# Zero matmuls in TensorE's early gaps, and the outer products of k moved from POOL to DVE, in a planned attention and token-mixing kernel

## The chip, the cores and the metric

The kernel runs on one core of a Trainium2 chip. The metric is the device time of one execution in microseconds, as the median of several runs. PE is the matrix engine TensorE, PEld its weight loads, DVE the vector engine, ACT the scalar engine, POOL the GpSimd engine and SP the queue that issues loads and stores.

## The reference

Four batches, four heads, 1088 positions, 32 features a head; sketch matrices of 8 rows.

```python
def phi(x):                                   # x: batch, head, position, 32
    a = einsum('rd,bhsd->bhsr', S1, x);  b = einsum('rd,bhsd->bhsr', S2, x)
    return einsum('bhsi,bhsj->bhsij', a, b)   # flattened to 64
q_p, k_p = phi(q), phi(k)
kv = einsum('bhsf,bhsd->bhfd', k_p, v);  z = k_p.sum(axis=2)
attn = einsum('bhsf,bhfd->bhsd', q_p, kv) / (einsum('bhsf,bhf->bhs', q_p, z) + 1e-6)
x = attn, heads side by side                  # batch, 1088, 128
theta = x @ w_theta
y = einsum('ts,bsd->btd', w_tok_r, x * cos(theta)) + einsum('ts,bsd->btd', w_tok_i, x * sin(theta))
u = x + y
out = u + relu(u @ w_ch)
```

The denominator can come close to zero, so it is computed in several levels of split numbers, while the numerator is plain float32. The weights arrive as 64-bit numbers, which the kernel turns into float32 itself.

## The kernel before, in words

Positions lie in nine chunks of 128, taken in three groups of three (`NG` = 3, `GC` = 3).

- For each batch, keys are cut into a bf16 grid and remainders (stages `grid`, `keys`, `sums`, `rest`). Sums over positions are formed on PE. For batch 0 DVE forms the remainders; for batches 1 to 3 POOL subtracts (L684), held back by a one-element tile `gate`, which is copied (L1106) when batch 0's factor `nu` is there. `chain` (L757), first for batch 0 and then for batches 1 to 3 together, goes back and forth between DVE (`split`, `split_t`, `cut`) and PE and gives the factors of the denominator.
- `kfeatures` (L701) makes the key features: PE transposes k (L714), ACT copies (L717), PE multiplies by the block matrix `sbk` into a PSUM tile `kf`, ACT copies all of it (192 columns) to SBUF as `ks` (L727), POOL forms the outer products `kp` chunk by chunk (36 instructions, `outer`, L731), and PE sums `kp` against v into `kv`. `chain_out` makes the block-diagonal tile `kvbd` from it.
- `query_scale`, `query_slices`, `levels` and `outputs_x` do the same for the queries: transposes, two slices of q, level products on PE, denominator on DVE (`den`), outer products of q (DVE for batch 0, POOL for batches 1 to 3, by `QPOOL`), numerator on PE (`num`), the phase with sine and cosine on ACT and the products with x on DVE into `z` (`theta`).
- The token weights come as 17 rows of 1088 columns. Each is loaded as 64-bit words, converted by three ACT instructions (L610, L612, L614) and put together by two DVE instructions (L616, L618).
- `mix_row` multiplies `z` by the rows on PE, 17 steps a group: batch 0 has its three groups at once and goes row by row; for batches 1 to 3 groups go one after another, with two groups of batch 1 early. `mix_out` adds x, applies the last weights and stores.

The order in which each engine gets its instructions is not the order of the source. Every operation is registered with `op(engine, duration, function, writes, reads, due)`. `Layout.run` goes backwards from the outputs' due times to give each operation a due time and adds a number for its stage from the table `SHIFT`. `Layout.forward` then plays the program with the written durations: of the operations that could start next on an engine it takes the one with the earliest due time, hands out buffer slots (of PSUM, class `ps`, there are eight, of which four are kept back for operations that are due earlier), and models that POOL and DVE hinder each other at a shared port (`lk`). `Layout.issue` emits the result in that order; each engine works through its queue strictly in it. A change of a duration, a shift or the rules can thus move every instruction of every engine.

Of the kernel before, what the change touches and what calls it, by code (L numbers as in the profile page):

```python
# [14 lines left out]
I32 = mybir.dt.int32  # L15
# [41 lines left out]
}  # L57
LOAD_LEAD = 60.0
RAW_LEAD = 30.0
CHAINS = ((0,), (1, 2, 3))  # L60
QPOOL = (False, True, True, True)
QFIX = 2.006
# [18 lines left out]
class Layout:  # L81


    START = {"P": 1.3, "V": 0.8, "A": 0.7, "G": 1.3, "S": 0.5}
    ISSUE = 0.4
# [71 lines left out]
    def forward(self):  # L157
# [21 lines left out]
        def place(o):  # L179
            t = 0.0  # L180
            need = {}
            for b in o.bufs:
                if b.slot is None and b.cls is not None:
                    need.setdefault(b.cls, []).append(b)
            for c, bs in need.items():
                av = sorted(s[0] for s in slots[c] if s[1] is None)
                last = max((b.due, b.ops[0]) for b in bs)
                before = bisect.bisect_left(pending[c], last, key=lambda x: x[:2]) - len(bs) + 1
                if len(av) < len(bs) + min(max(before, 0), self.RESERVE[c]):
                    return None  # L190
                t = max(t, av[len(bs) - 1])
            return t

        while done < len(ops):
            pick = None
            for e in "PVAGS":
                cand = []
                for o in ready[e]:
                    t = max(free[e], o.ready, o.due - o.lead)
                    p = place(o)  # L200
                    if p is None:
                        continue
                    t = max(t, p)
                    if o.lk:
# [7 lines left out]
                t, o = min((c for c in cand if c[0] <= first + self.SLACK[e]), key=lambda c: (c[1].rank, c[1].i))  # L212
                if pick is None or t < pick[0]:
                    pick = (t, o)
            if pick is None:
                raise RuntimeError("no room: " + str([(o.eng, round(o.due), [b.name for b in o.bufs]) for e in "PVAGS"
                                                      for o in ready[e]]))
# [38 lines left out]
    def issue(self, pools):  # L256
        for o in self.order:
            for b in o.bufs:
                if b.ap is None:
                    b.ap = view(pools[b.cls](b.slot), b.shape, b.dt)  # L260
            o.fn()
# [33 lines left out]
def kernel(  # L295
# [107 lines left out]
    op("V", 1.0, constants, [hm, bdm, halfpi, steps, ups, ones], [])  # L403
    op("A", 1.6, lambda: A.activation(warm(), halfpi(), AF.Sin), [warm], [halfpi], due=0.0)
# [13 lines left out]
    if wide:  # L418
# [4 lines left out]
        op("A", 0.4 * H + 0.4, read_small, [st], [], due=-9.0, fly=2.0)  # L423
# [86 lines left out]
    op("G", 1.3, sliced, [cm, c16, cf], [sc, sf], lk=7)  # L510
# [24 lines left out]
    op("G", 0.5, blocks_k, [s32, sbk], [sp, hm], lk=2)  # L535
# [40 lines left out]
    op("G", 0.9, spread2, [sx2, psc], [s0, sc], lk=4)  # L576
# [26 lines left out]
    def weight(dst, dfn, src, n, due=None):  # L603
# [8 lines left out]
        op("A", 0.24 + n * 0.00105, lambda: A.activation(stp()[:, :, 1].bitcast(F16), words_of(raw(), n)[1].bitcast(F32),  # L612
                                                     AF.Copy, scale=2.0**-60), [(stp, 1)], [raw])
        op("A", 0.24 + n * 0.00105, lambda: A.activation(stp()[:, :, 0], words_of(raw(), n)[0].bitcast(U32), AF.Copy,  # L614
# [3 lines left out]
        op("V", n * 0.0012 + 0.08, lambda: tt(V, dfn().bitcast(I32), dfn().bitcast(I32),  # L618
# [16 lines left out]
    def key_sums(b):  # L635
# [25 lines left out]
        op("V", 0.3, key_steps, [(km, 0)], [(km, 1), steps], lk=1)  # L661
# [11 lines left out]
        for c in range(NC):  # L673
            op("P", 0.22, lambda c=c: levels_of(c), [(t, "l")], [kb])
        at("rest", b)
        kh = buf("big", (NC, HD), F32, "kh")
        for g in range(NG):
            x = slice(g * GC, (g + 1) * GC)
            if b == 0:
                vop(GW, lambda x=x: tt(V, r()[:, x], r()[:, x], kb()[:, 1, x], ALU.subtract), [(r, g)], [(kb, 1)], lk=1)  # L680
                vop(GW, lambda x=x: stt(kh()[:, x], r()[:, x], -0.5, kx()[:, x].rearrange("p c h d -> p c (h d)"),
                                        ALU.mult, ALU.add), [(kh, g)], [(r, g), kx], lk=1)
            else:
                op("G", 0.93, lambda x=x: tt(G, r()[:, x], r()[:, x], kb()[:, 1, x], ALU.subtract), [(r, g)],  # L684
                   [(kb, 1), gate], lk=1)
# [15 lines left out]
    def kfeatures(b):  # L701
# [3 lines left out]
        for g in range(NG):  # L705
# [3 lines left out]
            ks = buf("sm", (CH, 2 * R), F32, "ks")  # L709
# [17 lines left out]
            op("A", act(CH * 2 * R), lambda kf=kf, ks=ks: A.copy(ks().rearrange("p n r -> p (n r)"), kf()), [ks], [kf])  # L727

            at("kv", b)

            def outer(i, kp=kp, ks=ks):  # L731
                h = slice(i * H, (i + 1) * H)
                tt(G, kp()[:, h], bc(ks()[:, h, 0:R], 3, [P, H, R, R]), bc(ks()[:, h, R:2 * R], 2, [P, H, R, R]), ALU.mult)

            for i in range(GC):
                op("G", 0.64, lambda i=i, f=outer: f(i), [(kp, i)], [ks, gate], lk=1)
# [20 lines left out]
    def chain(bs):  # L757
# [3 lines left out]
        for b in bs:  # L761
# [10 lines left out]
            op("V", 1.25, split, [e0, e1], [t, kg[b], kg[b, 0]], lk=1)  # L772
# [135 lines left out]
    def levels(b):  # L908
# [43 lines left out]
        op("V", 0.75, finish_den, [dn], [(ep[b], 1)], lk=2)  # L952
# [5 lines left out]
    def outputs_x(b, lv, pool_qp):  # L958
# [3 lines left out]
        for g in range(NG):  # L962
# [54 lines left out]
            op("A", act(GW) + .08, lambda cs=cs: A.activation(cs()[:, 0], cs()[:, 0], AF.Sin, bias=halfpi(),  # L1017
                                                              scale=-TWO_PI), [(cs, 0)], [halfpi])
            op("A", act(GW) + .08, lambda cs=cs: A.activation(cs()[:, 1], cs()[:, 1], AF.Sin, scale=-TWO_PI), [(cs, 1)],  # L1019
# [77 lines left out]
    for bs in CHAINS:  # L1097
# [34 lines left out]
    with tc.manual_schedule():  # L1132
        L.issue(pools)
# [43 lines left out]
```

## Time and profile before

| | |
|---|---|
| median of 3 runs | 283.65 us (283.55 to 283.65) |
| the profiled execution | 284.34 us, of which the span is 282.6 us |
| busy | PE 253.1, DVE 162.2, ACT 142.8, POOL 77.4 us |
| mean granted clock of PE | 0.962 |

A row of the profile names a line, an engine, an operation and the tiles it writes and reads. Buffers of one class have one name: `big`, `zs`, `g`, `sm`, `hf`, `lv` are classes of SBUF buffers and `ps` is PSUM. Helpers record their own line: L372 is every matmul, L356 every tensor-tensor operation on DVE or POOL, L360 every tensor-scalar and L363 every scalar-tensor-tensor; L714, L898, L982, L1004 and L1070 are transposes. A float32 matmul appears as two instructions.

### The profile page before, as it was taken

The numbers are of one execution on the slowest core, as the hardware profiler recorded it, in microseconds if no ns is written. First come the engines' busy times: TensorE is split into PE (matmuls) and PEld (weight loads), VectorE is DVE, ScalarE is ACT, GpSimd is POOL, SyncE is SP. The second block draws the span as 40 slices with busy tenths as digits, with TensorE's granted clock in tenths as the row PEclk, the third lists the DMA queues.
The fourth block names the chain that finished last, engine by engine and source line by source line (L and its number), as shares of the span: only waits on it lengthen the run. The fifth ranks groups of instructions, "written<-read, shape, count | busy, mean of one in ns | idle before, by whom it ended". The sixth has DMA issues, their size and how long they took to land.

```text
span 282.6 us, 3841 instructions
## 1 busy us (share of the span) xinstructions
PE 253.1 (90%) x1447; PEld 187.9 (67%) x1447; DVE 162.2 (57%) x337; ACT 142.8 (51%) x231; POOL 77.4 (27%) x112
## 2 busy tenths in 40 slices
PE   3596898588599899997999999999999999999993
PEld 3495797467497767664776687657876755565762
DVE  1768769999799999899564078104652400010102
ACT  4569953367667898977898040334606700000101
POOL 0291024999954800085000000700042000000000
PEclk9999557999989999999999999999999999999999
DMA  7999924406404018441500012000000000010011
GB/s 260 388 420 422 409 84 159 160 0 247 154 0 160 1 16 302 143 175 44 198 2 0 0 52 58 0 23 0 2 28 23 2 0 0 0 30 0 1 54 52
DMA packets 9154, 28.77 MB, mean 102 GB/s; under 512 B 944, under 2 KB 5296, under 8 KB 6960
## 3 DMA queue, kind: packets, MB, share of 16 engines
q1 hardware_dynamic: 8928, 28.51, 27.2%
q8 instruction: 11, 0.18, 0.3%
q14 instruction: 7, 0.06, 0.1%
q10 hardware_dynamic: 208, 0.02, 0.1%
HBM read 26.30 MB, written 2.23 MB: 101 GB/s over the span
## 4 chain that ended last, share of the span: by engine, by line
PE 61%; DVE 16%; POOL 9%; ACT 7%; issue 3%; DMA 2%; SPq 0%; DVEq 0%; ACTq 0%
PE ps L372 56%; POOL g L356 5%; DVE big L356 4%; POOL big L356 3%; DVE big L360 2%; DMA big<-q_l 2%; ACT big L614 2%; ACT big L612 2%; DVE lv L356 2%; PE ps L982 2%; DVE sm L356 2%; PE ps L1070 1%; DVE big L363 1%; ACT big L610 1%; PE ps L1004 1%
## 5 line engine op out<-in xcount | busy, mean ns | idle before, releaser
L372 PE MATMUL ps<-big,zs 128*128 128x384 f32 (+1 forms) x408 | 128.6, 469 | 0.0
L372 PEld LDWEIGHTS ps<-big,zs 128*128 128x128 f32 x408 | 75.6, 190 | 42.7 <-issue 0.8
L356 POOL TENSOR_TENSOR g<-lv 128x256 f32<-128x256 f32 x27 | 20.4, 790 | 95.9 <-DVE lv L356 95.9
L1080 ACT ACTIVATE g<-ps 128x384 f32<-128x384 f32 (+2 forms) x16 | 6.2, 406 | 65.8 <-PE ps L372 65.8
L356 POOL TENSOR_TENSOR g<-sm 128x256 f32<-128x256 f32 x36 | 35.6, 1024 | 6.7 <-ACT sm L727 6.7
L356 DVE TENSOR_TENSOR g<-big,ps 128x384 f32<-128x384 f32 (+1 forms) x12 | 6.4, 530 | 52.5 <-PE ps L372 52.5
L356 DVE CUSTOM_DVE_ANT_0 big<-big,big 128x2176 uint16<-128x2176 uint16 x17 | 23.9, 1404 | 5.1 <-ACT big L614 4.6
L612 ACT ACTIVATE big<-zs 128x1088 f16<-128x1088 f32 (+1 forms) x18 | 24.8, 1380 | 0.0
L614 ACT ACTIVATE big<-zs 128x1088 int16<-128x1088 uint32 (+1 forms) x18 | 24.8, 1376 | 0.0
L986 ACT COPY g<-ps 128x384 f32<-128x384 f32 x24 | 10.3, 483 | 22.3 <-PE ps L982 20.6
L610 ACT ACTIVATE big<-zs 128x1088 f32<-128x1088 f32 x17 | 20.5, 1213 | 0.6 <-DMA zs<-w_tok 0.6
L372 PE MATMUL ps<-big,big 128*128 128x128 f32 x72 | 11.4, 318 | 7.9 <-DVE big L363 7.8
L372 PEld LDWEIGHTS ps<-big,big 128*128 128x128 f32 x72 | 10.1, 222 | 9.0 <-DVE big L363 9.0
L356 DVE TENSOR_TENSOR zs<-ps,g 128x768 f32<-128x768 f32 (+2 forms) x20 | 12.0, 630 | 6.2 <-ACT g L1019 6.1
L360 DVE TENSOR_SCALAR big<-big 128x1088 int32<-128x1088 int32 x17 | 14.8, 869 | 1.1 <-ACT big L610 1.1
L363 DVE SCALAR_TENSOR_TENSOR g<-g,ps 128x384 f32<-128x384 f32 x12 | 6.6, 552 | 14.8 <-ACT g L1013 14.8
L356 DVE TENSOR_TENSOR g<-g,ps 128x384 f32<-128x384 f32 (+2 forms) x16 | 6.9, 450 | 14.0 <-ACT g L1080 9.0
L372 PE MATMUL ps<-mf,big 128*128 128x96 f32 x72 | 14.4, 295 | 0.5 <-DVE big L356 0.5
L372 PE MATMUL ps<-sbk,g 128*128 128x64 f32 x72 | 13.9, 359 | 0.8 <-POOL sbk L356 0.8
L372 PEld LDWEIGHTS ps<-sbk,g 128*128 128x128 f32 x72 | 13.1, 273 | 1.3 <-POOL sbk L356 0.9
L372 PE MATMUL ps<-g,big 128*64 128x128 f32 x144 | 11.4, 293 | 2.5 <-POOL g L356 2.5
L714 PE MATMUL ps<-ident,big 128*128 128x128 f32 x36 | 8.1, 389 | 4.8 <-DMA big<-k_l 4.8
(163 smaller groups left out, 391.8 us busy)
## 6 DMA issues: line engine op xcount, KB each, us to landing
zs<-w_tok SPq DMA_DIRECT2D x17, 1088.0 KB, 6.1
big<-k_l SPq DMA_DIRECT2D x4, 576.0 KB, 10.0
big<-v_l SPq DMA_DIRECT2D x4, 576.0 KB, 6.3
big<-q_l SPq DMA_DIRECT2D x4, 576.0 KB, 5.2
out<-g SPq DMA_DIRECT2D x8, 192.0 KB, 2.1
out<-g SPq DMA_DIRECT2D x4, 128.0 KB, 1.8
zs<-w_sq SPq DMA_DIRECT2D x1, 256.0 KB, 14.3
out<-g SPq DMA_DIRECT2D x4, 32.0 KB, 1.8
```

Source lines behind the costliest of these rows:

```text
L356: eng.tensor_tensor(out=o, in0=a, in1=b, op=f)
L360: (eng or V).tensor_scalar(out=o, in0=a, scalar1=s1, scalar2=s2, op0=op0, **kw)
L363: (eng or V).scalar_tensor_tensor(out=o, in0=a, scalar=s, in1=b, op0=op0, op1=op1)
L372: T.matmul(o, lhs, rhs, start=start, stop=stop, skip_group_check=True)
L610: op("A", 0.22 + n * 0.0009, lambda: A.activation(dfn(), words_of(raw(), n)[1].bitcast(F32), AF.Copy, scale=2.0**-112), [dst], [raw])
L612: op("A", 0.24 + n * 0.00105, lambda: A.activation(stp()[:, :, 1].bitcast(F16), words_of(raw(), n)[1].bitcast(F32), AF.Copy, scale=2.0**-6 ...
L614: op("A", 0.24 + n * 0.00105, lambda: A.activation(stp()[:, :, 0], words_of(raw(), n)[0].bitcast(U32), AF.Copy, scale=2.0**-29), [(stp, 0) ...
L714: T.transpose(tr()[:, i * P:(i + 1) * P], kx()[:, g * GC + i].rearrange("p h d -> p (h d)"), ident())
L982: T.transpose(tr()[:, i * P:(i + 1) * P], qp()[:, i * H + 2 * n:i * H + 2 * n + 2].rearrange("p h i j -> p (h i j)"), ident())
L986: op("A", act(GW), lambda n=n, tr=tr, qT=qT: A.copy(qT()[:, n], tr()), [(qT, n)], [tr])
L1004: T.transpose(x()[:, i], y_, ident())
L1080: op("A", act(m), lambda n=n, i0=i0, i1=i1, o=o: A.activation(o(), po()[:n, i0 * P:i1 * P], AF.Relu), [(ot, j)], [po])
```

## The change

- A tile of 384 bf16 zeros, `idle`, is written by POOL at the start. `spin` multiplies it by itself on PE into a PSUM tile `nowhere`. An operation with 11 of them is the first on PE; an operation with one, which reads batch 0's key-value block, is the last. Between these two, `issue` adds five of them for each planned microsecond of a gap on PE. `nowhere` holds one of the eight PSUM slots from the first to the last.
- The outer products of k go to DVE, one instruction of 128x768 for a group of three chunks (12 in all instead of 36). The first factor is the SBUF copy `ks`, now of 96 columns, the second is read from PSUM (`kf`). They do not wait for `gate`.
- `gate` is opened by the last write of batch 0's `cut` instead of by `nu`.
- Planner: POOL is looked at first; SP's operations no longer look at the port; if nothing has room, a second choice without kept-back slots is made; a dozen durations and three starting times are changed; the whole table `SHIFT` is new.

```diff
-    START = {"P": 1.3, "V": 0.8, "A": 0.7, "G": 1.3, "S": 0.5}
-    ISSUE = 0.4
+    START = {"P": 1.3, "V": 0.8, "A": 1.0, "G": 1.3, "S": 0.9}
+    ISSUE = 0.42
...
-            for e in "PVAGS":
+            for e in "GPVAS":
...
-    def issue(self, pools):
+    def issue(self, pools, fill, span):
+
+        last, on = 0.0, False
         for o in self.order:
+            if o.eng == "P":
+                if on:
+                    for _ in range(int((o.start - last - 0.08) * FILL)):
+                        fill()
+                last, on = o.end, on and o is not span[1] or o is span[0]
...
+    idle = fixed((GW,), BF16, "idle")
+    nowhere = buf("ps", (GW,), F32, "nowhere")
+
+    def spin():
+        T.matmul(nowhere(), idle()[:, 0:P], idle(), start=True, stop=True, skip_group_check=True)
+
+    op("G", 0.3, lambda: G.memset(idle(), 0.0), [idle], [], due=-20.0)
+    first = op("P", 3.2, lambda: [spin() for _ in range(11)], [nowhere], [idle], due=-10.0)
...
-            ks = buf("sm", (CH, 2 * R), F32, "ks")
+            ks = buf("sm", (CH, 2 * R if KPOOL[b] else R), F32, "ks")
...
+            fv = lambda kf=kf: kf().rearrange("p (n r) -> p n r", r=2 * R)
+            op("A", act(CH * 2 * R if KPOOL[b] else CH * R), lambda fv=fv, ks=ks: A.copy(ks(), fv()[:, :, 0:ks.shape[1]]),
+               [ks], [kf])
...
-            for i in range(GC):
-                op("G", 0.64, lambda i=i, f=outer: f(i), [(kp, i)], [ks, gate], lk=1)
+            if KPOOL[b]:
...
+            else:
+                vop(CH * R * R, lambda f=outer, fv=fv: f(V, slice(0, CH), fv), [kp], [ks, kf])
...
-            op("G", 0.1, lambda nu=nus[bs]: G.tensor_copy(gate(), nu()[:, 0, 0:1]), [gate], [nus[bs]], lk=1)
+            op("G", 0.1, lambda: G.tensor_copy(gate(), mf[0]()[:, 2, 0, 0:1]), [gate], [(mf[0], "y")], lk=1)
...
+        if not bs[0]:
+            last = op("P", 0.1, spin, [nowhere], [kvb[WARM]] if WARM < B else [idle])
```

Some of the shifts, before and after (smaller is earlier): `q00` 131.5 and -27.2, `levels0` 27.7 and -31.6, `den0` -154.1 and -48.2, `num0_0` -225.0 and -32.0, `theta0_0` -278.2 and -68.2, `sums1` 343.8 and -96.0, `sums3` 183.2 and -385.8, `rest1` -254.4 and -51.2, `keys3` 9.8 and -384.1, `row12` 50.4 and 74.8. `KPOOL` is False for every batch, `FILL` is 5.0, `WARM` 0.

More of the change, by code (lines that the diff above doesn't have):

```diff
@@ L34 @@
 SHIFT = {
[22 rows of a table removed]
-}
[22 rows of a table added]
+}
+WARM = 0
+FILL = 5.0
 LOAD_LEAD = 60.0
@@ L61 @@
 QPOOL = (False, True, True, True)
+KPOOL = (False, False, False, False)
+RPOOL = (False, True, True, True)
 QFIX = 2.006
@@ L177, in forward, with place @@
             v.sort(key=lambda x: x[:2])
-        def place(o):
+        def place(o, loose):
             t = 0.0
@@ L188, in place @@
                 before = bisect.bisect_left(pending[c], last, key=lambda x: x[:2]) - len(bs) + 1
-                if len(av) < len(bs) + min(max(before, 0), self.RESERVE[c]):
+                if len(av) < len(bs) + (0 if loose else min(max(before, 0), self.RESERVE[c])):
                     return None
@@ L192, in place, with choose @@
             return t
-        while done < len(ops):
+        def choose(loose):
             pick = None
-            for e in "PVAGS":
+            for e in "GPVAS":
                 cand = []
@@ L199, in forward @@
                     t = max(free[e], o.ready, o.due - o.lead)
-                    p = place(o)
+                    p = place(o, loose)
                     if p is None:
@@ L203, in forward @@
                     t = max(t, p)
-                    if o.lk:
+                    if o.lk and e != "S":
                         a, z, n = port["V" if e == "G" else "G"]
@@ L211, in forward @@
                 first = min(c[0] for c in cand)
-                t, o = min((c for c in cand if c[0] <= first + self.SLACK[e]), key=lambda c: (c[1].rank, c[1].i))
-                if pick is None or t < pick[0]:
+                t, o = min((c for c in cand if loose or c[0] <= first + self.SLACK[e]), key=lambda c: (c[1].rank, c[1].i))
+                if pick is None or (o.rank < pick[1].rank if loose else t < pick[0]):
                     pick = (t, o)
+            return pick
+        while done < len(ops):
+            pick = choose(False) or choose(True)
             if pick is None:
@@ L401, in constants @@
         V.memset(ones(), 1.0)
-    op("V", 1.0, constants, [hm, bdm, halfpi, steps, ups, ones], [])
-    op("A", 1.6, lambda: A.activation(warm(), halfpi(), AF.Sin), [warm], [halfpi], due=0.0)
+    idle = fixed((GW,), BF16, "idle")
[4 more added lines that the diff above has]
+    first = op("P", 3.2, lambda: [spin() for _ in range(11)], [nowhere], [idle], due=-10.0)
+    op("V", 1.25, constants, [hm, bdm, halfpi, steps, ups, ones], [])
+    op("A", 1.5, lambda: A.activation(warm(), halfpi(), AF.Sin), [warm], [halfpi], due=0.0)
     at("small")
@@ L422 @@
         op("V", 0.1, lambda: V.memset(st().bitcast(F32), 0.0), [st], [], due=-5.0)
-        op("A", 0.4 * H + 0.4, read_small, [st], [], due=-9.0, fly=2.0)
+        op("A", 0.52 * H + 0.52, read_small, [st], [], due=-9.0, fly=2.0)
         def words():
@@ L509 @@
     at("sliced")
-    op("G", 1.3, sliced, [cm, c16, cf], [sc, sf], lk=7)
+    op("G", 1.8, sliced, [cm, c16, cf], [sc, sf], lk=7)
     def tiny():
@@ L534 @@
     at("blocks_k")
-    op("G", 0.5, blocks_k, [s32, sbk], [sp, hm], lk=2)
+    op("G", 0.8, blocks_k, [s32, sbk], [sp, hm], lk=2)
     at("blocks_t")
@@ L574, in spread2 @@
         G.tensor_copy(psc()[:R, 1], sc()[:R, 0, 2 * R:])
-    op("G", 0.9, spread2, [sx2, psc], [s0, sc], lk=4)
+    op("G", 1.1, spread2, [sx2, psc], [s0, sc], lk=4)
     def prod2():
@@ L611, in weight @@
                                                      scale=2.0**-112), [dst], [raw])
-        op("A", 0.24 + n * 0.00105, lambda: A.activation(stp()[:, :, 1].bitcast(F16), words_of(raw(), n)[1].bitcast(F32),
+        op("A", 0.285 + n * 0.00105, lambda: A.activation(stp()[:, :, 1].bitcast(F16), words_of(raw(), n)[1].bitcast(F32),
                                                      AF.Copy, scale=2.0**-60), [(stp, 1)], [raw])
-        op("A", 0.24 + n * 0.00105, lambda: A.activation(stp()[:, :, 0], words_of(raw(), n)[0].bitcast(U32), AF.Copy,
+        op("A", 0.285 + n * 0.00105, lambda: A.activation(stp()[:, :, 0], words_of(raw(), n)[0].bitcast(U32), AF.Copy,
                                                      scale=2.0**-29), [(stp, 0)], [raw])
@@ L617, in weight @@
            [dst], [], lk=1)
-        op("V", n * 0.0012 + 0.08, lambda: tt(V, dfn().bitcast(I32), dfn().bitcast(I32),
+        op("V", n * 0.00112 + 0.08, lambda: tt(V, dfn().bitcast(I32), dfn().bitcast(I32),
                                           stp().rearrange("p n t -> p (n t)").bitcast(I32), ALU.add), [dst], [stp], due, lk=1)
@@ L659, in key_steps @@
             tt(V, km()[:, 0:2], steps(), km()[:, 3:4].to_broadcast([P, 2]), ALU.mult)
-        op("V", 0.3, key_steps, [(km, 0)], [(km, 1), steps], lk=1)
+        op("V", 0.36, key_steps, [(km, 0)], [(km, 1), steps], lk=1)
         at("keys", b)
@@ L673, in key_sums @@
         for c in range(NC):
-            op("P", 0.22, lambda c=c: levels_of(c), [(t, "l")], [kb])
+            op("P", 0.165, lambda c=c: levels_of(c), [(t, "l")], [kb])
         at("rest", b)
         kh = buf("big", (NC, HD), F32, "kh")
+        if b and not RPOOL[b]:
+            vop(n, lambda: tt(V, flat(r()), flat(r()), flat(kb()[:, 1]), ALU.subtract), [r], [(kb, 1)], lk=1)
         for g in range(NG):
@@ L682, in key_sums @@
                                         ALU.mult, ALU.add), [(kh, g)], [(r, g), kx], lk=1)
-            else:
+            elif RPOOL[b]:
                 op("G", 0.93, lambda x=x: tt(G, r()[:, x], r()[:, x], kb()[:, 1, x], ALU.subtract), [(r, g)],
@@ L726, in kfeatures, with outer @@
             op("P", 0.615, feats, [kf], [kT, sbk], hold=[ks])
-            op("A", act(CH * 2 * R), lambda kf=kf, ks=ks: A.copy(ks().rearrange("p n r -> p (n r)"), kf()), [ks], [kf])
+            fv = lambda kf=kf: kf().rearrange("p (n r) -> p n r", r=2 * R)
+            op("A", act(CH * 2 * R if KPOOL[b] else CH * R), lambda fv=fv, ks=ks: A.copy(ks(), fv()[:, :, 0:ks.shape[1]]),
+               [ks], [kf])
             at("kv", b)
-            def outer(i, kp=kp, ks=ks):
-                h = slice(i * H, (i + 1) * H)
-                tt(G, kp()[:, h], bc(ks()[:, h, 0:R], 3, [P, H, R, R]), bc(ks()[:, h, R:2 * R], 2, [P, H, R, R]), ALU.mult)
-            for i in range(GC):
-                op("G", 0.64, lambda i=i, f=outer: f(i), [(kp, i)], [ks, gate], lk=1)
+            def outer(E, h, y, kp=kp, ks=ks):
+                n = h.stop - h.start
+                tt(E, kp()[:, h], bc(ks()[:, h, 0:R], 3, [P, n, R, R]), bc(y()[:, h, R:2 * R], 2, [P, n, R, R]), ALU.mult)
+            if KPOOL[b]:
+                for i in range(GC):
+                    op("G", 0.64, lambda i=i, f=outer, ks=ks: f(G, slice(i * H, (i + 1) * H), ks), [(kp, i)], [ks, gate],
+                       lk=1)
+            else:
+                vop(CH * R * R, lambda f=outer, fv=fv: f(V, slice(0, CH), fv), [kp], [ks, kf])
             def sums(g=g, kp=kp):
@@ L770, in split @@
                 tt(V, e1(), t()[:, 2], e1(), ALU.add)
-            op("V", 1.25, split, [e0, e1], [t, kg[b], kg[b, 0]], lk=1)
+            op("V", 1.4, split, [e0, e1], [t, kg[b], kg[b, 0]], lk=1)
         tp = buf("ps", (nb, 2, HR), F32, "tp")
@@ L950, in finish_den @@
             V.reciprocal(dn()[:, 1], dn()[:, 0])
-        op("V", 0.75, finish_den, [dn], [(ep[b], 1)], lk=2)
+        op("V", 0.8, finish_den, [dn], [(ep[b], 1)], lk=2)
         vop(NT, lambda: tt(V, lv()[:, 0].rearrange("p (n r) -> p n r", r=R),
@@ L1016, in outputs_x @@
             op("A", act(GW), lambda cs=cs: A.activation(cs()[:, 0], cs()[:, 1], AF.Abs), [(cs, 0)], [(cs, 1)])
-            op("A", act(GW) + .08, lambda cs=cs: A.activation(cs()[:, 0], cs()[:, 0], AF.Sin, bias=halfpi(),
+            op("A", act(GW) + .12, lambda cs=cs: A.activation(cs()[:, 0], cs()[:, 0], AF.Sin, bias=halfpi(),
                                                               scale=-TWO_PI), [(cs, 0)], [halfpi])
-            op("A", act(GW) + .08, lambda cs=cs: A.activation(cs()[:, 1], cs()[:, 1], AF.Sin, scale=-TWO_PI), [(cs, 1)],
+            op("A", act(GW) + .12, lambda cs=cs: A.activation(cs()[:, 1], cs()[:, 1], AF.Sin, scale=-TWO_PI), [(cs, 1)],
                [])
@@ L1132 @@
     with tc.manual_schedule():
-        L.issue(pools)
+        L.issue(pools, spin, (first, last))
 def kernel(q, k, v, S1, S2, moe_w_theta, moe_w_tok_r, moe_w_tok_i, moe_w_ch):
```

44 rows, old and new, of the table SHIFT are left out of this document.

## The prediction

> **What bounds the kernel now.** I read the busy shares first, then the 40 slices, then stretches of my own, then the chain of waits, and last the single engines' rows.
>
> ```profile
> span 282.6 us, 3841 instructions
> PE 253.1 (90%) x1447; PEld 187.9 (67%) x1447; DVE 162.2 (57%) x337; ACT 142.8 (51%) x231; POOL 77.4 (27%) x112
> PE   3596898588599899997999999999999999999993
> PEclk9999557999989999999999999999999999999999
> 4.75:21.70 16.95, 13.66 (x63) 12.81 (x64) 10.24 (x41) 11.58 (x22) 8.93 (x31) 1.00 1.01 399
> 29.50:46.05 16.55, 15.51 (x73) 14.19 (x74) 12.45 (x37) 11.39 (x20) 3.10 (x6) 0.50 0.56 214
> 47.27:102.97 55.70, 45.39 (x440) 39.00 (x440) 53.17 (x77) 36.24 (x59) 43.71 (x40) 0.97 0.26 93
> 101.00:133.50 32.50, 30.65 (x155) 21.22 (x155) 30.41 (x67) 28.06 (x35) 9.76 (x9) 1.00 0.42 142
> 133.50:277.80 144.30, 144.25 (x696) 98.37 (x697) 48.21 (x91) 47.87 (x92) 10.61 (x18) 1.00 0.07 25
> ```
>
> The columns of a stretch are its length, the busy time of PE, PEld, DVE, ACT and POOL, the granted clock, the DMA share and GB/s. From 133.5 us on PE is never free (144.25 of 144.30): nothing there can be won except by PE having less left to do. All that can be won lies before. Between 101 and 133.5 PE loses 1.9 us; between 47.27 and 102.97 it loses 10.3 us, while DVE is busy 53.17 of 55.70 us: there DVE is what PE waits for. Before 46 us PE is slow, which the busy share hides:
>
> ```profile
> 4.75 2.15 PE L714 MATMUL ps<-ident,big 128*128 128x128 f32 x9 [4.75 <-DMA big<-k_l]
> 84.01 1.20 PE L714 MATMUL ps<-ident,big 128*128 128x128 f32 x9
> L372 PE MATMUL ps<-sbk,g 128*128 128x64 f32 x18 | 4.1, 424 | 0.8 <-POOL sbk L356 0.8
> L372 PE MATMUL ps<-sbk,g 128*128 128x64 f32 x18 | 2.2, 269 | 0.0
> 19.99 0.85 PE L372 MATMUL ps<-big 128*128 128x256 bf16 x4
> 21.91 1.30 PE L372 MATMUL ps<-big 128*128 128x256 bf16 x12
> 76.21 3.68 PE L372 MATMUL ps<-big,big 128*128 128x128 f32 x18 [3.37 <-DVE big L363]
> 62.34 2.23 PE L372 MATMUL ps<-big,big 128*128 128x128 f32 x18
> ```
>
> The first of each pair is early or after a pause, the second the same work at another time: nine transposes 2.15 against 1.20 us, eighteen feature matmuls 4.1 against 2.2 us. So the 1.00 shown for 4.75 to 21.7 us isn't what PE ran at: it ran at half speed until about 21.7 us, when bf16 matmuls fall from 0.21 to 0.11 us each, at full speed to 29.5, and by the granted clock of 0.50 at half speed again until 46.05. After the pause of 3.37 us at 72.8 it is slow once more, for some 4 us.
>
> **The change, part by part.** The chain of waits says what of this counts:
>
> ```profile
> 1.63 6.46 DMA big<-q_l
> 30.73 2.09 PE ps L372 x8
> 33.73 2.61 PE ps L372 x10
> 36.41 3.56 PE ps L372 x16
> 47.27 5.60 POOL big L356 x5
> 58.45 13.20 POOL g L356 x13
> 71.65 2.71 POOL big L356 x3
> 74.38 1.77 DVE big L363
> ```
>
> Fillers. A list of 11 bf16 matmuls of 128x384 zeros goes first on PE, and then five per planned microsecond of gap until batch 0's key-value block is done. At 0.21 us for 256 columns one takes an estimated 0.32 us slow, 11 take 3.5 us. They lie in the 4.75 us in which PE waits for k, and may overrun it by some tenths, which the chain hides behind the load of q. If they keep PE fast, PE's pieces on the chain before 46 us shrink: 2.09, 2.61 and 3.56 make 8.26 us. They consist of small matmuls with a wait after each, so I take not half but 0.6 of their time, between the feature pair's 0.54 and no gain at all where ACT or DVE ends last: **-3.3 us**, bounds 0 and -3.8. The earlier feature piece (4.1 us) could give 1.9 us more, so -5.7 at most; but the chain goes from it into row conversions on ACT, so it is costed at nothing. Cover for the fillers' own time is PE's planned gap; where work comes sooner than planned it queues behind fillers of an estimated 0.14 to 0.32 us each: **+0.3 us**, bounds 0 and 2. They hold one of eight PSUM banks.
>
> Here the Trainium skill speaks against. Its page "TensorE: Matmul & The Clock Gate", Part 1, says that the clock ramp is under 1% of a typical span, and Part 4 that a transpose does not count as PE-busy the way a matmul does. By the first this term would be capped near 2.8 us; this trace shows three slow stretches instead of one ramp. With the second the trace agrees so far, as 13.66 us of work full of transposes before 21.7 us did not raise the speed. The transposes at 84.01 do run fast once PE is fast.
>
> Outer products of k. On POOL they are 36 instructions, on DVE 12:
>
> ```profile
> L356 POOL TENSOR_TENSOR g<-sm 128x256 f32<-128x256 f32 x36 | 35.6, 1024 | 6.7 <-ACT sm L727 6.7
> L356 DVE TENSOR_TENSOR zs<-ps,g 128x768 f32<-128x768 f32 x6 | 5.6, 955 | 4.1 <-ACT g L1019 4.1
> L356 DVE TENSOR_TENSOR g<-lv 128x768 f32<-128x768 f32 x3 | 2.8, 953 | 0.0
> ```
>
> Of the same size, with a PSUM factor or with broadcast ones, DVE takes 0.955 us: 12 of them put 11.5 us on DVE, which has 2.5 us free between 47.27 and 102.97. In exchange DVE's other work gets shorter where POOL is no longer at it. First 0 to 47 us, then 47 to 98 us:
>
> ```profile
> L360 DVE TENSOR_SCALAR big<-big,sm 128x1152 bf16<-128x1152 f32 x5 | 4.4, 873 | 0.0
> L356 DVE TENSOR_TENSOR big<-big,big 128x1152 f32<-128x1152 f32 x3 | 4.1, 1351 | 0.1
> L356 DVE CUSTOM_DVE_ANT_0 big<-big,big 128x2176 uint16<-128x2176 uint16 x3 | 3.9, 1285 | 0.6 <-ACT big L614 0.6
> L360 DVE TENSOR_SCALAR big<-big 128x1088 int32<-128x1088 int32 x3 | 2.1, 716 | 0.0
> ...
> L356 DVE CUSTOM_DVE_ANT_0 big<-big,big 128x2176 uint16<-128x2176 uint16 x5 | 8.0, 1602 | 0.1
> L363 DVE SCALAR_TENSOR_TENSOR big<-big,big 128x1152 f32<-128x1152 f32 x3 | 5.6, 1869 | 1.4 <-POOL big L356 1.4
> L360 DVE TENSOR_SCALAR big<-big 128x1088 int32<-128x1088 int32 x6 | 5.6, 930 | 0.0
> L360 DVE TENSOR_SCALAR big<-big,sm 128x1152 bf16<-128x1152 f32 x4 | 4.4, 1090 | 0.1
> ```
>
> The excess is 5 x 0.317 + 3 x 0.518 (against the tensor-tensor of that size) + 6 x 0.214 + 4 x 0.217 = 5.3 us on 23.6 us of such work, 22%. On the 53.17 us of DVE work in the stretch that would be up to 12 us. Of the 40 POOL instructions there, nine are the subtractions and 31 outer products of k, 31 x 1.024 = 31.7 of 43.71 us, so nearly three quarters of the excess goes with them: 4 us at least, 9 at most; I take 8, since the rows not shown are slowed likewise. Net on DVE +3.5, less the 2.5 us that DVE stood idle, mostly for POOL's subtractions (the step to 74.38): **+1.0 us**, bounds -2 (relief 9, all idle time back) and +7.5 (relief 4, no idle time back). POOL's 21 us on the chain vanish, but what is late next is DVE, already full there; hence no gain of 21 us. The product reads one factor from PSUM, so that bank waits for DVE's turn instead of ACT's copy. ACT copies 96 instead of 192 elements, off the chain: nothing. The three subtractions per batch stay on POOL, behind a gate that now opens at the end of batch 0's cut instead of in its middle; behind it stand only those subtractions, the first of which the chain has at 47.27, released by DVE's slices and not by the gate: nothing.
>
> Order. New shifts and durations put all engines' queues in another order. No row of before shows it, so I bound it:
>
> ```profile
> 97.14 1.81 DVE L356 TENSOR_TENSOR zs<-ps,g 128x768 f32<-128x768 f32 x2
> 102.97 7.56 PE L372 MATMUL ps<-big,zs 128*128 128x384 f32 x24
> 76.90:80.75 3.85, 3.85 (x29) 3.63 (x29) 3.75 (x5) 0.78 (x2) 3.85 (x5) 0.57 0.00 0
> ```
>
> Mixing begins at 102.97, when batch 0's phases have come from DVE at 97.14. What PE can regain until then is its 10.3 us idle between 47.27 and 102.97 and some 1.7 us of the slow stretch: 12 us if batch 0 is done earlier and rows are there. At the other end nothing excludes a loss, since another order can open other waits; the 1.9 us that PE loses between 101 and 133.5 are the nearest row for such waits, so +2. The shifts speak both ways: the slices of q for batch 0 move up (131.5 to -27.2), the values' remainders of batch 1 move back (-254.4 to -51.2), but phases of batch 0 too (-278.2 to -68.2), and the sums of keys 1 to 3 move up by 440 and more. I take half: **-6 us**.
>
> Sum: 284.34 us of the profiled execution (span 282.6 and 1.7 us around it) - 3.3 + 0.3 + 1.0 - 6 = 276.3. The runs' median is 0.7 us below that execution: **275.6, said as 275.5 us**.
>
> **The rivals.**
> First, the order gives all: PE, fast and without the pause at 72.8 us, gets batch 0's mixing from about 90 us on and no idle is left in the middle. Then -12 stands for -6, and with -5.7 for the first term the time is 267 us, by more freed idle at the end of the range 264. For it: PE's 10.3 us idle are real, and keys of other batches and rows share DVE there with batch 0. Against: DVE must still do the rows and has 11.5 us more.
>
> Second, nothing gained: DVE, full from 47 us, sets the end whatever PE's speed before, and the early gain is eaten by the net 3.5 us on DVE. -3.3 + 0.3 + 3.5 leaves 284.1 after the 0.7. For it: 53.17 of 55.70. Against: DVE is idle for about 4 us between 29.5 and 46.05 (12.45 of 16.55), in which a product may go.
>
> Third, **slower**: POOL's place taken by DVE as a bound. If the relief is 4 us and the idle time does not return, DVE carries +7.5 us between 47 and 103; with the order worth nothing, 284.34 - 3.3 + 0.3 + 7.5 - 0.7 = 288 us. It decides from where relief and early gain together are below the 11.5 us added, that is relief under about 8.5 (11.5 + 0.3 - 3.3) with none of the order's gain. For it: rivals for DVE's time, row conversions above all, remain. Against: the k products are needed late for batches 1 to 3.
>
> Fourth, the fillers don't do what they say: the 3.5 us of them miss, transposes follow, and PE stays slow until denser work. Then the first term is gone: 275.6 + 3.3 = 279 us. For it: the rows before 21.7 us. Against: later gaps are filled too.
>
> **How the numbers follow.** The forecast (270 to 281 us, its own range) has 0.50, the first rival 0.20, the second 0.12, the third 0.10, the fourth 0.08. The second is shared between no change, 0.05, and a little either way. Faster by over 0.2% (0.6 us, about what runs of this kernel can tell): 0.83; within it 0.05; slower 0.12. 264 to 285 us leaves out the third rival and the far end of the first, under 2 in 10.
>
> **What would show it.** Fillers: nine k transposes at about 1.2 us from the first batch on, granted clock 1.00 from about 8 us on, no 0.50 at 30 to 46. Outer products: 12 DVE rows of 128x768 near 0.95 us, POOL's busy time down from 77.4 to about 40 us, the row combine near 1.3 us instead of 1.6 between 47 and 98. Order: the first mixing matmul of 128x384 earlier than 102.97 by 6 us or more beyond PE's early gain, and PE's lasting saturation before 133.5. It is wrong if DVE's busy share stays at 95% up to the same 133 us with PE waiting for it, or if PE's waits for DVE grow in the first 60 us since a PSUM bank is held.

## The result, and the profile after

The changed kernel takes 275.03 us (median of 4 runs, 272.4 to 275.84), the kernel before 283.6; the ratio is 0.9688, interval 0.9617 to 0.9758. The profiled execution took 274.38 us. Here and below, ratios and their intervals leave out single executions that ran over 1.5% longer than the fastest of their kernel at a lower clock; the medians keep them. First the page of the profiled execution, then the stretches that were shown of before and the last one from where PE is saturated (length, busy time of PE, PEld, DVE, ACT, POOL, clock, DMA share, GB/s).

```profile
span 272.6 us, 3960 instructions
PE 256.5 (94%) x1518; PEld 185.5 (68%) x1518; DVE 162.8 (60%) x349; ACT 143.5 (53%) x231; POOL 46.7 (17%) x77
PEclk9999999997999599999999999999999999999998
L422 PE MATMUL ps<-idle 128*128 128x384 bf16 x71 | 15.6, 365 | 1.3 <-POOL idle L424 1.3
```

```profile
4.75:21.70 16.95, 15.16 (x117) 12.07 (x117) 13.10 (x38) 12.75 (x27) 0.00 (x0) 1.00 1.00 391
29.50:46.05 16.55, 16.55 (x171) 14.46 (x170) 14.03 (x39) 10.65 (x18) 7.51 (x22) 1.00 0.43 160
47.27:102.97 55.70, 50.68 (x398) 41.12 (x396) 51.85 (x112) 43.51 (x65) 7.58 (x6) 0.91 0.32 107
118.00:267.80 149.80, 149.62 (x699) 101.70 (x700) 59.19 (x98) 58.78 (x95) 16.58 (x18) 1.00 0.13 43
```

PE is never free from 118 us on instead of from 133.5. The clock of 0.50 between 30 and 46 us is gone. By PE's account the whole gain looks like the clock: its own work fell from 253.1 to 256.5 - 15.6 = 240.9 us, while its idle time with the zeros in it went from 29.5 to 31.7. The experiments show that the zeros are not what brings the gain.

PE's rows in order of time (start, length, what; in brackets the wait before):

```profile
1.33 3.70 PE L422 MATMUL ps<-idle 128*128 128x384 bf16 x11 [1.33 <-POOL idle L424]
4.85 1.51 PE L739 MATMUL ps<-ident,big 128*128 128x128 f32 x6
7.32 2.60 PE L422 MATMUL ps<-idle 128*128 128x384 bf16 x15
11.79 1.20 PE L928 MATMUL ps<-ident,big 128*128 128x128 f32 x9 [1.00 <-DMA big<-q_l]
95.74 7.63 PE L387 MATMUL ps<-big,zs 128*128 128x384 f32 x24
```

The eleven zeros take 3.7 us, the transposes of k behind them are still slow (0.25 us each), those of q at 11.79 fast (0.13). Mixing starts 7.2 us earlier than before (102.97). DVE from 47 to 98 us by shape:

```profile
L371 DVE TENSOR_TENSOR g<-sm,ps 128x768 f32<-128x768 f32 x6 | 5.7, 943 | 0.0
L371 DVE CUSTOM_DVE_ANT_0 big<-big,big 128x2176 uint16<-128x2176 uint16 x4 | 5.2, 1288 | 0.1
L375 DVE TENSOR_SCALAR big<-big 128x1088 int32<-128x1088 int32 x4 | 2.9, 718 | 0.0
L378 DVE SCALAR_TENSOR_TENSOR big<-big,big 128x1152 f32<-128x1152 f32 x2 | 2.7, 1354 | 0.0
```

An outer product takes 0.943 us, and in that stretch DVE's other instructions are back at their unhindered lengths: 1.288 us for the row combine instead of 1.602, 1.354 for the scalar-tensor-tensor instead of 1.869.

### The profile page after: what moved, and what is told of

The parts are those of the page before. It is cut to its first block, busy times and chain, and to the rows that moved or that the text cites. A ratio compares the mean times of both kernels' runs of the same rounds, so it can differ in the third digit from the quotient of the medians.

```text
span 272.6 us, 3960 instructions
## 1 busy us (share of the span) xinstructions
PE 256.5 (94%) x1518; PEld 185.5 (68%) x1518; DVE 162.8 (60%) x349; ACT 143.5 (53%) x231; POOL 46.7 (17%) x77
## 4 chain that ended last, share of the span: by engine, by line
PE 72%; DVE 17%; DMA 4%; ACT 3%; issue 2%; DVEq 0%; SPq 0%; ACTq 0%
PE ps L387 64%; DVE big L371 3%; PE ps L1012 2%; DVE big L375 2%; DMA big<-q_l 2%; DVE lv L371 2%; DVE g L371 2%; DVE big L378 1%; PE ps L1100 1%; DMA big<-k_l 1%; PE ps L422 1%; DVE sm L371 1%; PE ps L1034 1%; DVE sm L375 1%; PE ps L928 1%
## 5 line engine op out<-in xcount | busy, mean ns | idle before, releaser
L371 POOL TENSOR_TENSOR g<-lv 128x256 f32<-128x256 f32 x27 | 26.9, 1031 | 107.4 <-DVE lv L371 74.8
L371 DVE CUSTOM_DVE_ANT_0 big<-big,big 128x2176 uint16<-128x2176 uint16 x17 | 23.9, 1408 | 2.7 <-ACT big L637 1.8
L387 PE MATMUL ps<-mf,big 128*128 128x96 f32 x72 | 17.1, 335 | 0.0
L422 PE MATMUL ps<-idle 128*128 128x384 bf16 x71 | 15.6, 365 | 1.3 <-POOL idle L424 1.3
L371 POOL TENSOR_TENSOR big<-big,big 128x384 f32<-128x384 f32 x9 | 10.2, 1163 | 20.3 <-PE ps L1012 14.9
L1012 PE MATMUL ps<-ident,g 128*128 128x128 f32 x72 | 10.7, 289 | 2.8 <-DVE g L371 1.5
L1012 PEld LDWEIGHTS ps<-ident,g 128*128 128x128 f32 x72 | 8.6, 148 | 6.7 <-POOL g L371 2.3
L387 PEld LDWEIGHTS ps<-mf,big 128*128 128x128 f32 x72 | 12.9, 225 | 0.0
L387 PE MATMUL ps<-g,sm 128*64 128x384 f32 x48 | 11.6, 536 | 0.2 <-ACT g L1016 0.2
L387 PE MATMUL ps<-mv,hf 128*128 128x96 f16 x108 | 11.7, 223 | 0.0
```

The costliest lines, as they stand in the source:

```text
L371: eng.tensor_tensor(out=o, in0=a, in1=b, op=f)
L387: T.matmul(o, lhs, rhs, start=start, stop=stop, skip_group_check=True)
L422: T.matmul(nowhere(), idle()[:, 0:P], idle(), start=True, stop=True, skip_group_check=True)
L1012: T.transpose(tr()[:, i * P:(i + 1) * P], qp()[:, i * H + 2 * n:i * H + 2 * n + 2].rearrange("p h i j -> p (h i j)"), ident())
```

## The experiments

Two orders, fillers or not, outer products of k on DVE or on POOL: eight kernels, each keeping the instruction order of its parent. "Order" means everything of the change except fillers and move: shifts, durations, the planner's rules and the gate. Medians in us; beside each stood the kernel before, at 283.5 to 283.9.

| order | neither | fillers | move | both |
|---|---|---|---|---|
| of before | 283.6 | 279.83 | 286.29 | 282.33 |
| of the change | 285.95 | 286.68 | 273.35 | 273.66 and 275.03 |

### The change without fillers

```diff
-    first = op("P", 3.2, lambda: [spin() for _ in range(11)], [nowhere], [idle], due=-10.0)
+    first = op("P", 3.2, lambda: [spin() for _ in range(1)], [nowhere], [idle], due=-10.0)
...
-                        fill()
+                        pass
```

> The changed kernel with its order on every engine kept, but without fillers: no zeros in the planned gaps and one instead of eleven at the start. Theory C (the clock carries the gain): PE's own work, 240.9 us with fillers, goes back to about 252 us, with the slow stretches before 46 us back, and the time to 281 to 284 us. Theory P (the prediction's sum: the fillers are worth 3.0 us, the order 6): about 278 us. Theory O (order and outer products alone): 275 us, as the changed kernel.

Measured: 273.35 us, ratio 0.9633 (0.9599 to 0.9666). The unaltered change in another set of runs gave 273.66 us, ratio 0.9656 (0.9616 to 0.9696). The two intervals overlap: in this order the fillers are worth nothing that these runs can tell. Theory O is nearest, C and P are out. PE's rows without fillers, and the gate's row on POOL:

```profile
4.57 1.51 PE L739 MATMUL ps<-ident,big 128*128 128x128 f32 x6 [2.73 <-DMA big<-k_l]
11.19 2.18 PE L928 MATMUL ps<-ident,big 128*128 128x128 f32 x9 [0.84 <-DMA big<-q_l]
26.07 1.18 PE L928 MATMUL ps<-ident,big 128*128 128x128 f32 x9
39.72 0.19 POOL L1136 COPY gate<-mf 128x1 f32<-128x1 f32 x1 [3.55 <-DVE mf L378]
```

PE is slow at 11 us, fast at 26, and the granted clock is 1.00 from there to 79 us without a zero. The end of batch 0's cut, which the gate's copy on POOL marks, comes at 39.72 without and at 39.69 us with fillers: what PE saves there is covered by the other engines. Theory C's sign did not come either: PE is busy 245.6 us and not 252. Before it was 253.1, and with fillers its own work is 240.9, so more than half of that fall comes without the zeros.

### The list at the start alone

```diff
-                        fill()
+                        pass
```

> The changed kernel with the eleven zeros at the start and none in the gaps. Fourth rival of the prediction (the list at the start misses, transposes do not keep PE fast): the clock falls to half soon after the start and stays there for most of the time to 40 us; time as without fillers, 278 to 284 us. Theory that the list alone is enough once PE is fast: 275 us and PE at full speed from 5 to 46 us.

Measured: 274.27 us, ratio 0.9659 (0.9624 to 0.9695). Part of the fourth rival is there, PE slow again behind the list, but its price is not:

```profile
4.68 0.82 PE L739 MATMUL ps<-ident,big 128*128 128x128 f32 x6
10.51 0.59 PE L387 MATMUL ps<-sm,ones 128*128 128x1 f32 x2 [4.01 <-ACT big L667]
10.96 2.16 PE L928 MATMUL ps<-ident,big 128*128 128x128 f32 x9
```

After the list the first six transposes run fast here (in the changed kernel's profile, with the same list, slow), PE then waits 4.0 us for its next work, and the next nine are slow again.

### Outer products of k back on POOL

```diff
-                vop(CH * R * R, lambda f=outer, fv=fv: f(V, slice(0, CH), fv), [kp], [ks, kf])
+                vop(CH * R * R, lambda f=outer, ks=ks: [f(G, slice(i * H, (i + 1) * H), ks) for i in range(GC)], [kp], [ks, kf])
```

`ks` has 192 columns again. With fillers:

> The changed kernel, fillers kept, with the outer products of k back on POOL at the same places of the order: 36 POOL instructions of 256 elements, both factors from SBUF, ACT copying 192 columns again. Theory P: the move cost 1.0 us net, so 274 us. Theory C says the same place doesn't matter much: 274 to 277. Rival K (the move itself carries the gain, since POOL is slow and hinders DVE): 280 us or more, with DVE's row combine back near 1.6 us in the stretch where POOL works on k.

and without:

> The changed kernel's order alone: no fillers, and the outer products of k on POOL at the same places. Theory P: 283.6 - 6 = 277.6 us. Theory C: the order alone gives nothing or little, 281 to 285 us. Theory O: 275 to 277 us.

Measured: 286.68 us (ratio 1.0091, 1.0058 to 1.0125) and 285.95 us (1.0066, 1.0038 to 1.0095). In the first only rival K's number holds; in the second theory C's is nearest, though the fillers are not its reason. Without the move the new order is slower than the old one, and the move is worth 12.6 us in it. That POOL hinders DVE, one of rival K's two reasons, does not explain it: without fillers DVE is busy 158.1 us with the products on POOL and 162.8 us with the move, so the move gives DVE more to do. What POOL's rows show is a queue. First the run without fillers, and below it the row for `sbt` of the run with the move, also without fillers:

```profile
28.60 5.18 POOL L371 TENSOR_TENSOR g<-sm 128x256 f32<-128x256 f32 x6
33.74 0.44 POOL L371 TENSOR_TENSOR sbt<-sq,hm 128x32 f32<-128x32 f32 x2
44.53 0.19 POOL L1136 COPY gate<-mf 128x1 f32<-128x1 f32 x1 [3.44 <-DVE mf L378]
```

```profile
29.01 0.88 POOL L371 TENSOR_TENSOR sbt<-sq,hm 128x32 f32<-128x32 f32 x2 [0.21 <-DVE sq L371]
```

Six products stand ahead of the blocks `sbt` that batch 0's chain needs; they come at 33.74 instead of 29.01 us, 4.7 us later, and the cut ends at 44.53 instead of 39.72, 4.8 us later.

### Only batch 0's outer products on DVE

```diff
-                vop(CH * R * R, lambda f=outer, fv=fv: f(V, slice(0, CH), fv), [kp], [ks, kf])
+                vop(CH * R * R, (lambda f=outer, ks=ks: [f(G, slice(i * H, (i + 1) * H), ks) for i in range(GC)]) if b else
+                    (lambda f=outer, fv=fv: f(V, slice(0, CH), fv)), [kp], [ks, kf])
```

> The changed kernel's order without fillers, outer products of k on DVE for batch 0 alone and on POOL for batches 1 to 3, at the same places. With all of them on POOL it took 285.95 us, with all on DVE 273.35. Theory Q (POOL's queue: batch 0's nine products stand ahead of the blocks that batch 0's chain needs): most of the loss goes, 274 to 278 us. Theory L (POOL's load and its contention with DVE from 46 to 95 us): 281 to 285 us.

Measured: 280.09 us, ratio 0.9852 (0.9813 to 0.9891): about half of the 12.6 us, between the two theories. The cut ends at 40.83 us, 3.7 us earlier than with all products on POOL, so most of batch 0's share is the queue ahead of its chain. The rest comes later, as the stretch from 39.7 to 72 us shows, first without fillers and all products on DVE, then this kernel:

```profile
39.70:72.00 32.30, 28.88 (x286) 24.63 (x286) 30.91 (x47) 24.50 (x40) 10.37 (x10) 1.00 0.26 88
39.70:72.00 32.30, 26.06 (x246) 21.45 (x246) 24.44 (x42) 21.68 (x32) 19.68 (x26) 0.95 0.27 93
```

With the products of batches 1 to 3 on POOL, DVE is busy 24.4 of 32.3 us instead of 30.9: it is not overloaded by POOL, it stands waiting. In POOL's queue the products alternate with the subtractions, and DVE waits for these; the last two rows are DVE's waits in the stretch (total in us, times, longest), in this kernel and with all products on DVE:

```profile
41.84 1.80 POOL L371 TENSOR_TENSOR g<-sm 128x256 f32<-128x256 f32 x3
43.59 0.92 POOL L371 TENSOR_TENSOR big<-big,big 128x384 f32<-128x384 f32 x1
44.46 1.80 POOL L371 TENSOR_TENSOR g<-sm 128x256 f32<-128x256 f32 x3
```

```profile
DVE big L378 <- POOL big L371: 6.2, 2, 4.3
```

```profile
DVE big L378 <- POOL big L371: 0.8, 1, 0.8
```

The wait of 6.2 us instead of 0.8 is most of the 6.5 us by which DVE is less busy.

### The move in the old order

```diff
-                tt(G, kp()[:, h], bc(ks()[:, h, 0:R], 3, [P, H, R, R]), bc(ks()[:, h, R:2 * R], 2, [P, H, R, R]), ALU.mult)
+                tt(V, kp(), bc(ks()[:, :, 0:R], 3, [P, CH, R, R]), bc(ks()[:, :, R:2 * R], 2, [P, CH, R, R]), ALU.mult)
```

It is issued once a group, at the place of the group's first POOL instruction, both factors from SBUF.

> The kernel before with one thing changed: the outer products of k on DVE, 12 instructions of 768 elements at the place of each group's first POOL instruction, both factors from SBUF; order otherwise kept, no fillers. Prediction's term for the move: +1.0 us (bounds -2 and +7.5), so 284 to 285 us, DVE's row combine back near 1.3 us. Theory K (the move carries the gain by itself): 273 to 277 us. Theory M (move and order only work together): 279 to 285 us.

Measured: 286.29 us, ratio 1.0092 (1.0065 to 1.0118), within the prediction's bounds for the term, 1.4 us above its value. The page of this run, and the stretch that was shown of before:

```profile
PE 253.1 (89%) x1447; PEld 189.4 (67%) x1447; DVE 163.3 (57%) x349; ACT 142.5 (50%) x231; POOL 44.0 (15%) x76
47.27:102.97 55.70, 43.28 (x405) 38.41 (x405) 52.13 (x85) 34.06 (x55) 11.65 (x8) 0.91 0.26 92
```

DVE's total rose by 1.1 us though 11.3 us were added: 10.2 us came back. Yet PE got less done in the stretch, 43.28 instead of 45.39 us, at a clock of 0.91 instead of 0.97. POOL's part of the chain was replaced by DVE's, as the prediction had it. The sign expected of the row combines did not come: their five in 47 to 98 us still average 1.527 us, since two of them (1.78 and 2.00 us) run beside the subtractions that stay on POOL.

### Fillers in the old order

```diff
+        last, on, n0 = None, True, 11
...
+                gap = n0 if last is None else int((o.start - last - 0.08) * FILL)
+                if on and gap > 0:
...
+                        dst = pools["ps"](min(free)[1])[:, 0:384]
+                        for _ in range(gap):
+                            fill(dst)
```

The zeros are written to a PSUM bank that is free at that place.

> The kernel before with one thing changed: fillers as in the change (eleven at the start, five per planned microsecond of gap until batch 0's key-value block), order kept, written to free PSUM banks. Prediction's term: -3.0 us, so 280.5 us, with PE fast from about 5 to 60 us. Theory D (PE's early slowness is covered by other engines): 283 to 285 us.

Measured: 279.83 us, ratio 0.9853 (0.9829 to 0.9878): -4.1 us against the prediction's -3.0. The chain of waits shows it as it was reasoned:

```profile
42.34 5.60 POOL big L373 x5
53.52 13.20 POOL g L373 x13
98.06 10.29 PE ps L389 x61
128.63 3.02 PE ps L389 x18
```

These four pieces were at 47.27, 58.45, 102.99 and 133.55 us. Everything behind PE's early pieces moves 4.9 us earlier in this profile, POOL's steps unchanged in length. The three pieces that the prediction named take 1.17, 1.08 and 1.96 us instead of 2.09, 2.61 and 3.56.

### Fillers and move in the old order

> The kernel before with fillers and with the outer products of k on DVE, order kept: the change without its order. Alone the fillers gave 4.1 us and the move cost 2.4. Additive: 282 us. Theory D: with DVE as the bound in the middle the early gain of the fillers is kept, as it comes before 47 us: 281 to 283 us. If fillers and move are all that matter and the order nothing: 274 us.

The edit is that of the last two together. Measured: 282.33 us, ratio 0.9952 (0.9934 to 0.997). The parts add: -4.1 and +2.4 from 283.6 are 281.9. Without the new order the change would have been worth 0.5%.

### The outer products twice

```diff
-                vop(CH * R * R, lambda f=outer, fv=fv: f(V, slice(0, CH), fv), [kp], [ks, kf])
+                vop(CH * R * R, lambda f=outer, fv=fv: [f(V, slice(0, CH), fv) for _ in range(2)], [kp], [ks, kf])
```

On the changed kernel without fillers.

> The changed kernel without fillers (273.35 us) with each of the 12 outer products of k done twice on DVE, order kept: some 11 us more on DVE, all before 82 us, nothing else. Theory D (DVE sets the end until 118 us): 281 to 285 us. Theory E (PE or the transfers set it, DVE only looks full): 274 to 276 us.

Measured: 286.77 us, ratio 1.0108 (1.0073 to 1.0143): 13.4 us more for this:

```profile
L371 DVE TENSOR_TENSOR g<-sm,ps 128x768 f32<-128x768 f32 x24 | 22.6, 949 | 0.4
```

It is 11.4 us more than the 11.2 of the changed kernel. All of it and 2 us more reach the end, beyond theory D's 281 to 285 us; the 2 us were not separated, but PE's mean clock is lower, 0.946 instead of 0.986. Mixing begins at 107.77 us instead of 94.25, so the loss is there before PE is saturated. In the new order DVE sets the pace until then.

### More fillers

```diff
+                elif gap > 0 and span[1].end < o.start < FILL_TO:
+                    free = [(t, s) for s, (t, b) in held.items() if not left[b]]
+                    if free:
+                        dst = pools["ps"](min(free)[1])[:, 0:384]
+                        for _ in range(gap):
+                            fill(dst)
```

> The changed kernel with 63 more fillers, in the planned gaps between the end of batch 0's key-value block and 120 us, written to whatever PSUM bank is free there; order kept. Theory C (PE's speed sets the end once it is full): the slow stretches at 62 to 66 and 89 to 96 us vanish, they hold some 10 us of slow work, so up to 5 us less: 268 to 270 us. Theory D (DVE sets the end until 118 us, so PE's speed before that is cover): the slow stretches vanish too and the time stays at 273 to 276 us.

Beside it the unaltered change:

> The changed kernel unaltered, beside the next three on one chip: 272 to 276 us, with the time falling as the mean granted clock rises. If the fillers are worth nothing (run without them: 273.35 us), it is not faster than 273 us here.

Measured: 274.98 us (ratio 0.968, 0.964 to 0.9721) and 273.66 us (0.9656, 0.9616 to 0.9696). The stretches of 60 to 67 and 88 to 97 us, first of the unaltered change and then with more fillers:

```profile
60.00:67.00 7.00, 5.54 (x31) 3.65 (x30) 6.21 (x9) 5.03 (x11) 1.15 (x1) 0.76 0.45 159
88.00:97.00 9.00, 8.65 (x58) 7.34 (x59) 8.45 (x30) 5.70 (x10) 0.00 (x0) 0.81 0.08 31
60.00:67.00 7.00, 6.79 (x56) 4.07 (x53) 6.72 (x13) 5.94 (x11) 0.00 (x0) 1.00 0.47 159
88.00:97.00 9.00, 8.74 (x78) 6.51 (x77) 8.23 (x36) 4.57 (x8) 0.00 (x0) 1.00 0.28 114
```

The slow clock of both stretches is gone and the time is no shorter: theory D.

### A few fillers at three places

Zeros only before three instructions: 6 and 6 around 60 us, 11 at 87 us.

> The changed kernel with no fillers but 23 zeros at three places where its PE pauses and then runs slow: 6 and 6 around 60 us, 11 at 87 us before batch 1's first level products; order kept. Theory D: the slow stretch at 89 to 96 us shrinks by up to 3 us, but DVE has under 3 us free until 118 us: 271 to 273.5 us, at best a little under the changed kernel. Theory C: 270 us or less.

Measured: 274.61 us, ratio 0.9673 (0.9647 to 0.9698), above what either theory gave. In the profiled run mixing starts at 92.74 us, 1.5 us before the kernel without fillers; then DVE's token-weight rows are not there:

```profile
103.75 3.99 PE L402 MATMUL ps<-big,zs 128*128 128x384 f32 x6 [3.35 <-DVE big L386]
```

The next mixing matmuls wait 3.35 us for a row (2.53 without fillers) and then run at a granted clock of 0.50: six take 3.99 us instead of 2.10. So one slow stretch was traded for another behind the next pause. No version tried beats the change clearly; the one without fillers is as fast and simpler.

## Why the prediction was right or wrong

The time (275.5 against 275.03) came out right by luck, as two errors cancel. Fillers were put at -3.0 us and are worth nothing in the new order; order and move were put at -5 together and brought -10.2 (283.52 to 273.35). Two terms held for the old order, but the change's gain lies in how order and move act on each other, and a sum of terms has no place for that.

Fillers, -3.0 us: right in the old order (-4.1), by the mechanism named, PE's pieces before 46 us on batch 0's chain. They shrank to about half, not to 0.6. Wrong for the change, where they are worth nothing. The failed step is that pieces on the chain of before would be on the chain after; the bound "no gain at all where ACT or DVE ends last" was the case. The nine fast transposes "from the first batch on" did not show either: the list made the first six fast in one profile and not in another. A zero took 0.17 us when PE was fast, not the lower estimate of 0.14.

Move, +1.0 us: in the old order +2.4. The 11.5 us were right (11.2 to 11.3), and so was the relief of 8. DVE's instructions come in the same order in both profiles; those that lie between 47.27 and 102.97 us in the kernel before take 8.3 us less in sum with the move, and those ahead of them 1.0 us less. (The 10.2 us of the totals is more, since instructions that overlap count once there.) What failed is the idle time: DVE is still idle for 3.6 us of that stretch (52.13 of 55.70), so the 2.5 us that the term took off did not come back as work. The lower bound of -2 does not follow from its own terms either: 11.5 - 9 - 2.5 is 0. What else the old order paid for was not separated. The Trainium skill's page "SBUF — State Buffer" states under "SBUF: two separate sides" that GpSimd shares a port pair with those DVE instructions that have two SBUF inputs or run in a 2-port mode, and that whichever starts first holds it for its whole instruction while the other waits. The rows agree in kind: row combines, which read two SBUF tiles, take 0.31 us longer beside POOL on average, and 1.288 us in the changed kernel's stretch, where POOL is idle beside them. Over the whole run they take 23.9 us before and after, as others of them now run beside POOL's products of q.

Order, -6 us: alone it is +2.4, with the move -12.9 (286.29 to 273.35). This term failed in its nature. It was bounded by what PE could regain in its idle time, with a half taken, and not asked which engine's queue the new order was made for. It is an order for a POOL without the products of k: with them in it, batch 0's cut ends 4.8 us later (44.53 against 39.72), and DVE waits for the subtractions behind them. With the move both are free. That makes the move worth 12.6 us in this order; the statement that POOL's 21 us on the chain bring no gain because DVE is late next is true for the old order alone. Two things stay open: which part of the new order does this, and what the planner would make of the new shifts if it planned with the products on POOL, since the runs above only put them at places planned for DVE.

Rivals: the first one's -12 for the order is near the -12.9 measured with the move, but not for its reason, since PE's early speed is not needed for it. The second and third (DVE the bound) have the mechanism that rules the changed kernel, since doubling the products costs their full time, but from a level 10 us lower. Of the fourth, the slow PE behind the list shows in single profiles, without its price.

What would show it: mixing started 7.2 us earlier, which is 6 us or more beyond an early gain of nothing, and PE was saturated from 118 us on. POOL's busy time fell to 46.7 us and not to about 40, mostly because its 27 products of q took 26.9 us instead of 20.4. The clock was not 1.00 from 8 us on: it fell to 0.76 around 60 to 67 us and to 0.81 around 88 to 97 us in a profile of the changed kernel.

## What to carry to other kernels

A change of placement and a change of order should be priced together: test each in the other's absence before adding terms, since here two parts that each lose 2.4 us alone gain 10 us together. A share of slow clock is worth something only where the engine is on the chain; an accounting of PE's busy time gave all the gain to the clock, and taking the fillers out took none of the gain away. When an engine's busy work leaves its queue, look at what stood behind it, not only at how long it took.

## What the runs showed of the hardware

PE's speed after the same start differed between executions: behind the same eleven zeros of 3.5 to 3.7 us, six transposes took 0.82 us in one profile and 1.51 in another (fillers at the start alone, and the changed kernel). The Trainium skill's page "TensorE: Matmul & The Clock Gate", Part 1, says that activity is judged in a free-running window of about 3.4 us, so that the moment of the rise shifts from run to run; both profiles agree with that. Part 4 of that page of the Trainium skill states that the full clock does not engage for transposes, as they don't count as busy in the same way. The rows show that transposes do run at full speed once PE is fast: nine took 1.20 us, 0.13 us each, against 0.25 us each when it was slow. Whether transposes alone would raise the clock no run here shows.
